# Global queries' scores in fp16 pairs: 32 columns of the array for each head

## The chip, the cores and the metric

The kernel runs on one core of a Trainium2 chip. The metric is device microseconds of one execution. The kernel before takes 972.75 us, the median of three runs (970.81 to 973.52).

## The reference

Attention with 8 batches, 8 heads, 512 local and 32 global positions of 64 elements, and behind it a feed-forward part with the function g = h * tanh(softplus(h)):

```python
k_all = np.concatenate([k_g, k_l], axis=2)
v_all = np.concatenate([v_g, v_l], axis=2)
s_g = scale * np.matmul(q_g, k_all.transpose(0, 1, 3, 2))   # 32 global queries against all 544 keys
out_g = np.matmul(sm(s_g), v_all)
s_ll = np.where(mask, scale * np.matmul(q_l, k_l.transpose(0, 1, 3, 2)), -1e9)   # |i - j| <= 32
s_lg = scale * np.matmul(q_l, k_g.transpose(0, 1, 3, 2))
out_l = np.matmul(sm(np.concatenate([s_lg, s_ll], axis=-1)), v_all)
x = np.concatenate([out_g, out_l], axis=2)      # as (8 * 544, 512)
h = x @ w_in                                    # 512 to 2048
out = (h * np.tanh(np.log1p(np.exp(h)))) @ w_out   # 2048 to 512
```

Here `sm` is the softmax. The change touches `s_g` alone: the scores of the 32 global queries of a head against its 32 global and 512 local keys.

## The kernel before

Heads go in pairs: 8 batches by 4 pairs are 32 head pairs `(b, hp)`. A pair's work is cut into four *units* of 128 local queries; in the third unit (`t == 2`) the global queries of the pair are worked as well. Beside the attention run the two products of the feed-forward part: `h` (line 869, 12 matmuls of 256 columns for half a step) and `o` (line 937, 6 of 512 columns). A block of 256 rows has eight such steps; 17 blocks make 136 steps.

fp32 operands are split into a high and a low fp16 part, so that a product of fp32 accuracy is a sum of fp16 matmuls. For the first eight head pairs (batches 0 and 1) the scores are taken straight from fp32 instead (`plain_s`). For the other 24 the keys are there as `ks` (high) and `kl` (low), and the queries hold the high part in one half of the partitions and the low part in the other, so that one matmul over 128 partitions gives two of the partial products.

The 24 sets of global scores are made by `g_scores` (from line 771), in two parts that go into two banks: part 0 has 32 columns of global keys and 256 of local ones, part 1 has 256 local ones. The stationary operand is a slice of `qgh`, whose 64 columns are 32 for either head; in the slice for head 0 the columns of head 1 are zeros, and the other way round. All four products (high and low keys, two heads) are added up in one region of 64 partitions: 0 to 31 for head 0, 32 to 63 for head 1. So a part has 4 matmuls for every range of columns, and a head pair 12: 8 of 256 columns and 4 of 32.

What follows a set: the row maximum (`g_max`, VectorE, line 791), Exp (`g_exp`, ScalarE, line 799), the normalized and split probabilities `gph` (VectorE, lines 807 to 811), a DMA transpose into `gpt` (line 482) and the product with the values `gu` (line 826).

No engine's order is written out by hand. Each piece of work is a task with the engine or engines that may do it, a duration in ns and what it reads and writes. `Plan.order` runs through the tasks with these durations, in priority order, and so fixes each engine's queue and, where two engines can do a task, which of them does it. A task of another table of functions (Exp or Mish) on ScalarE carries an `ACT_TABLE_LOAD`. The durations of `g_scores` are the second argument of its `pl.add(PE, ...)`, where `mm(n, cols)` stands for n matmuls of that many columns.

Of the kernel before, what the change touches and what calls it, by code (L numbers as in the profile page):

```python
# [48 lines left out]
PE, DVE, ACT, POOL, DMA = "PE", "DVE", "ACT", "POOL", "DMA"  # L49
# [174 lines left out]
def attn_mish_kernel(ctx: ExitStack, tc: tile.TileContext, qt, kt, qt0, kt0, mxs, vm, vg, qg, w1, w2, consts_in, out, w64):  # L224
    nc = tc.nc
    V, A, T, G = nc.vector, nc.scalar, nc.tensor, nc.gpsimd
# [17 lines left out]
    pl = Plan()  # L244
    X = pl.tile
# [44 lines left out]
    def mm(n, cols):  # L290
        return n * max(28, cols / 2.4)
# [175 lines left out]
    def plain_s(b, hp):  # L467
        return b * HP + hp < NPS

    def pair(b, hp, kind):  # L470

        return (kind, b, hp // 2), hp % 2
# [97 lines left out]
    def loc(k, j, n):  # L570

        a = k[:, 160 * j:160 * j + 64]
        return bass.AP(a.tensor, a.offset, [list(a.ap[0]), [160, n], [96, 2], list(a.ap[-1])])
# [54 lines left out]
    def bank(name):  # L628

        return [("h" if early else "sc", name)]  # L630
# [140 lines left out]
    def g_scores(b, hp, part):  # L771
        ks, kl, q, g = ("ks", b, hp), ("kl", b, hp), ("qgh", b), ("g", b, hp, part)

        def products(terms):
            a = 0 if part else 32
            for c0, n, rhs in ((a, 256, lambda k: loc(k, 2 * part, 2)), (0, 32, lambda k: k[:, GC:GC + 32]))[:2 - part]:
                for i, (a, k) in enumerate(terms):
                    T.matmul(X[g][:64, c0:c0 + n], a, rhs(k), start=(i == 0), stop=(i == len(terms) - 1))  # L778

        if plain_s(b, hp):  # L780
            kn, kp = pair(b, hp, "kn")
            pl.add(PE, mm(1, 1024) + 150 + (1 - part) * 90, lambda: products([(X["qgraw", b][:, 0, hp, :], X[kn][:, kp])]),
                   r=[[kn, kp], ("qgraw", b)], new=bank(g))
            return
        pl.add(PE, mm(4, 262) + 100 + (1 - part) * 110, lambda: products([(X[q][:, h, hp, :], X[k][:, h]) for k in (ks, kl) for h in range(2)]),
               r=[ks, kl, q], new=bank(g))

    def g_max(b, hp):
# [197 lines left out]
    def slot(u):  # L986
# [43 lines left out]
        if t == 2:  # L1030
            att(g_scores, b, hp, 0)
            att(g_scores, b, hp, 1)
            att(g_max, b, hp)
# [122 lines left out]
    for x in ORDER.split():  # L1156
        a, n = x[0], int(x[1:] or 0)
# [92 lines left out]
```

## Time and profile before

| | |
|---|---|
| median of three runs | 972.75 us |
| the profiled execution | 970.08 us, span 968.3 us |
| TensorE (PE) busy | 924.9 us, 96% |
| VectorE (DVE) busy | 677.3 us, 70% |
| ScalarE (ACT) busy | 660.2 us, 68% |
| mean granted TensorE clock | 0.979 |
| first and last start of a matmul of the 24 blocks | 213.5 and 812.3 us |

Line numbers are those of the listing above; PE is TensorE's matmuls, PEld its weight loads, which overlap them. A group's row gives the tiles and shapes, the count, the time in which any of them ran, the mean of one, and the idle time of the engine just before them. A shape such as `128*64 128x256` is a matmul over 128 partitions with 64 columns of weights that streams 256 columns.

### The profile page before, as it was taken

How to read it: one execution, taken by the hardware profiler on the slowest of the kernel's cores; microseconds unless marked ns; L12 is line 12 of the kernel's file. 1: busy time of each engine (PE TensorE's matmuls, PEld its weight loads, DVE VectorE, ACT ScalarE, POOL GpSimd, SP SyncE). 2: the span in 40 equal slices, each digit the busy share in tenths (PEclk: the TensorE clock that was granted, in tenths of full speed). 3: DMA queues.
4: the chain of work that ended last, by engine and by line, in shares of the span. 5: the costliest groups of instructions: out<-in, count | busy, mean ns of one | idle time of the engine just before them, and what ended most of it. 6: DMA issues, size and time to landing. Idle time of an engine off the chain costs nothing.

```text
span 968.3 us, 20617 instructions
## 1 busy us (share of the span) xinstructions
PE 924.9 (96%) x7988; PEld 644.6 (67%) x7988; DVE 677.3 (70%) x1782; ACT 660.2 (68%) x1301; POOL 15.8 (2%) x28
## 2 busy tenths in 40 slices
PE   6787999999999999999999999999999999999995
PEld 3554774667677677676777777777677777666663
DVE  6799989778899788766777778776777655322221
ACT  4657677687788788787878887878888887211110
POOL 2000000000000000000000000000000000000000
PEclk9977899999999999999999999999999999999998
DMA  8887549888999867756585676565767442100000
GB/s 271 245 299 220 151 118 211 192 184 227 236 220 250 168 137 189 162 139 130 135 171 132 145 163 146 131 138 123 187 119 155 75 101 52 34 1 23 1 22 22
DMA packets 214010, 141.00 MB, mean 146 GB/s; under 512 B 176664, under 2 KB 188184, under 8 KB 212888
## 3 DMA queue, kind: packets, MB, share of 16 engines
q1 hardware_dynamic: 213912, 139.69, 60.0%
q8 instruction: 62, 1.02, 0.5%
q14 instruction: 36, 0.29, 0.1%
HBM read 75.15 MB, written 8.91 MB: 87 GB/s over the span
## 4 chain that ended last, share of the span: by engine, by line
PE 70%; DVE 15%; DMA 8%; issue 2%; ACT 2%; SPq 1%; POOL 0%; DVEq 0%; ACTq 0%
PE h L869 28%; PE o L937 27%; DMA pt<-ph 3%; PE U L740 3%; PE g L778 3%; DMA gpt<-gph 3%; PE s L656 3%; PE s L649 2%; DVE P L662 2%; PE gu L826 1%; DMA vraw<-in_vm 1%; DVE G L925 1%; DVE W L407 1%; DVE W L459 1%; DVE vmx L497 1%
## 5 line engine op out<-in xcount | busy, mean ns | idle before, releaser
L937 PE MATMUL o<-W,G 128*128 128x512 f16 x1632 | 390.1, 380 | 0.0
L869 PE MATMUL h<-xh,W 128*128 128x256 f16 x2048 | 376.7, 273 | 2.2 <-ACT e L912 2.2
L869 PEld LDWEIGHTS <-W 128*128 128x128 f16 x3264 | 311.2, 98 | 66.5 <-issue 8.9
L869 PE MATMUL h<-xl,W 128*128 128x256 f16 x1024 | 279.6, 273 | 0.0
L937 PEld LDWEIGHTS <-G 128*128 128x128 f16 x1632 | 158.0, 98 | 148.2 <-issue 4.2
L912 ACT ACTIVATE e<-h,c 128x512 f32<-128x512 f32 (+1 forms) x137 | 92.6, 683 | 124.8 <-PE h L869 123.6
L671 ACT ACTIVATE P<-P,nm 128x192 f32<-128x192 f32 (+1 forms) x256 | 117.9, 461 | 42.6 <-DVE nm L662 39.6
L328 DVE TENSOR_SCALAR G<-e,c 128x512 f16<-128x512 f32 (+1 forms) x117 | 56.1, 481 | 118.2 <-ACT e L912 118.1
L662 DVE CUSTOM_DVE_ANT_0 P<-s,consts 128x192 f32<-128x192 f32 (+1 forms) x256 | 91.1, 367 | 57.1 <-PE s L656 50.6
L925 DVE SCALAR_TENSOR_TENSOR G<-e,c,G 128x512 f16<-128x512 f32 (+1 forms) x137 | 101.9, 744 | 2.6
L723 DVE SCALAR_TENSOR_TENSOR ph<-P,ph 128x384 f16<-128x384 f32 (+1 forms) x112 | 65.4, 585 | 49.1 <-ACT ph L326 48.6
L912 ACT ACT_TABLE_LOAD x74 | 94.9, 1283 | 1.3
L671 ACT ACT_TABLE_LOAD x66 | 84.7, 1283 | 1.2
L740 PEld LDWEIGHTS <-pt 96*128 96x128 f16 (+1 forms) x1536 | 62.4, 99 | 15.3 <-DMA pt<-ph 5.3
L326 ACT ACTIVATE ph<-P 128x384 f16<-128x384 f32 (+1 forms) x107 | 58.3, 546 | 8.6 <-DMA pt<-ph 5.8
L740 PE MATMUL U<-va,pt 128*128 128x64 f16 (+1 forms) x768 | 57.3, 195 | 4.1 <-DMA pt<-ph 3.2
L740 PE MATMUL U<-vc,pt 96*128 96x64 f16 x768 | 56.2, 194 | 0.0
L671 ACT ACTIVATION_READ_ACCUMULATOR P<-P,nm 128x1 f32 x256 | 47.9, 187 | 0.0
L799 ACT ACTIVATE gP<-g,gmx 64x288 f32<-64x288 f32 x64 | 30.3, 475 | 24.8 <-DVE gmx L794 24.6
L656 PEld LDWEIGHTS <-qs 128*128 128x128 f16 x384 | 34.9, 98 | 17.2 <-issue 0.9
L649 PE MATMUL s<-kn,qn 64*128 64x192 f32 (+1 forms) x128 | 37.2, 486 | 7.6 <-DMA qn<-in_qt 4.4
L656 PE MATMUL s<-ks,qs 128*128 128x192 f16 (+1 forms) x192 | 42.3, 254 | 0.2 <-ACT gP L799 0.2
(121 smaller groups left out, 961.4 us busy)
## 6 DMA issues: line engine op xcount, KB each, us to landing
kraw<-in_kt SPq DMA_DIRECT2D x24, 640.0 KB, 4.3
kn_m<-in_mxs SPq DMA_DIRECT2D x24, 544.0 KB, 4.8
qraw<-in_qt SPq DMA_DIRECT2D x24, 512.0 KB, 4.3
out<-ob SPq DMA_DIRECT2D x34, 256.0 KB, 2.4
vraw<-in_vm SPq DMA_DIRECT2D x8, 1024.0 KB, 6.0
wraw<-in_w SPq DMA_DIRECT2D x16, 512.0 KB, 5.0
W<-in_w SPq DMA_DIRECT2D x16, 512.0 KB, 6.7
vc<-vf SPq DMA_DIRECT2D x32, 128.0 KB, 2.4
```

What stands on the lines that cost most here:

```text
L326: A.activation(out=dst, in_=src, func=AF.Copy, scale=c)
L328: V.tensor_scalar(dst, src, c, None, ALU.mult)
L649: pl.add(PE, mm(1, 4 * w), lambda: T.matmul(X[s][:, :w], X[q][r, part, t * 128:(t + 1) * 128], X[k][r, part, c0:c0 + w], start=True, stop= ...
L656: T.matmul(X[s][:, :w], X[qs][:, h, t * 128:(t + 1) * 128], X[k][:, h, c0:c0 + w], start=(i == 0), stop=(i == 1))
L662: pl.add(DVE, 69 + 1.04 * w, lambda: V.tensor_tensor_reduce(out=X[P][:, h, :w], in0=X[s][:, :w], in1=mask[:, m0:m0 + w], scale=-SCALE, sca ...
L671: pl.add(ACT, 94 + 0.832 * w + 186, lambda: A.activation(out=X[P][:, h, :w], in_=X[P][:, h, :w], func=AF.Exp, bias=X[nm], scale=-1.0, accu ...
L723: pl.add(DVE, dve(n), lambda: V.scalar_tensor_tensor(p_part(X[ph], t, 1), p_src(X[P], t), PSC, p_part(X[ph], t, 0), ALU.mult, ALU.subtract ...
L740: T.matmul(X[u][:, t, h, :], X[pt][:k, p * 4 + h * 2 + c, :], X[vx][:k, t, vl, h * 64:(h + 1) * 64], start=(n == 0), stop=(n == 5))
L869: T.matmul(X[h][:, f * TB:(f + 1) * TB], wh(i, wl)[:, off:off + 128], X[x][:, d, o:o + TB], start=(n == 0), stop=(n == 11))
L912: chain(blk, i, ACT, 587, lambda a, z: A.activation(out=X[e][:, a:z], in_=hv(blk, i)[:, a:z], func=AF.Mish, bias=0.0, scale=X[c][:, 0:1]), ...
L925: chain(blk, i, DVE, 663, lambda a, z: V.scalar_tensor_tensor(gp(1, blk, i)[:, a:z], X[e][:, a:z], X["c", blk][:, 2:3], gp(0, blk, i)[:, a ...
L937: T.matmul(X[o], gp(g, blk, i)[:, f, t * 128:(t + 1) * 128], wh(8 + i, wl)[:, f * 512:(f + 1) * 512], start=(i == 0 and n == 0), stop=(i = ...
```

## The change

For the 24 fp16 head pairs, a head's products go to its own 32 columns of the array and its own 32 partitions of the bank, with only the 32 columns of `qgh` that hold that head's queries. They are issued in turns: high keys for head 0, high keys for head 1, low keys for head 0, low keys for head 1, for each range of columns. Each head's pair of products is a sum of its own with its own `start` and `stop`. The number of matmuls and weight loads stays the same, as does the tile `qgh`. The eight fp32 pairs issue what they issued before. The planner's durations for the two fp16 parts are changed with it.

```diff
-        def products(terms):
+        def products(*groups):
             a = 0 if part else 32
             for c0, n, rhs in ((a, 256, lambda k: loc(k, 2 * part, 2)), (0, 32, lambda k: k[:, GC:GC + 32]))[:2 - part]:
-                for i, (a, k) in enumerate(terms):
-                    T.matmul(X[g][:64, c0:c0 + n], a, rhs(k), start=(i == 0), stop=(i == len(terms) - 1))
+                for i in range(len(groups[0][2])):
+                    for p0, p1, terms in groups:
+                        a, k = terms[i]
+                        T.matmul(X[g][p0:p1, c0:c0 + n], a, rhs(k), start=(i == 0), stop=(i == len(terms) - 1))
...
-            pl.add(PE, mm(1, 1024) + 150 + (1 - part) * 90, lambda: products([(X["qgraw", b][:, 0, hp, :], X[kn][:, kp])]),
+            pl.add(PE, mm(1, 1024) + 150 + (1 - part) * 90, lambda: products((0, 64, [(X["qgraw", b][:, 0, hp, :], X[kn][:, kp])])),
                    r=[[kn, kp], ("qgraw", b)], new=bank(g))
             return
-        pl.add(PE, mm(4, 262) + 100 + (1 - part) * 110, lambda: products([(X[q][:, h, hp, :], X[k][:, h]) for k in (ks, kl) for h in range(2)]),
+        pl.add(PE, mm(2, 262) + 160 + (1 - part) * 80, lambda: products(*(
+            (h * 32, h * 32 + 32, [(X[q][:, h, hp, h * 32:h * 32 + 32], X[k][:, h]) for k in (ks, kl)]) for h in range(2))),
                r=[ks, kl, q], new=bank(g))
```

On TensorE, the first of the 24 blocks and what stands behind it. Before (`g_0_1` is part 1 of the head pair; rows in which both orders agree are left out):

```order
L778 LDWEIGHTS qgh_2695
L778 MATMUL g_0_1_2780<-kl_0_1909,qgh_2695 64x256
L937 LDWEIGHTS G_2605
L937 MATMUL o_0_2169<-W,G_2605 128x512
...
L869 LDWEIGHTS W
L869 MATMUL h_0_2804<-xh_1902,W 128x256
L869 LDWEIGHTS W
L869 MATMUL h_0_2804<-xl_1915,W 128x256
```

The same place with the change:

```order
L780 LDWEIGHTS qgh_2695
L780 MATMUL g_0_1_2780<-kl_0_1909,qgh_2695 32x256
L940 LDWEIGHTS G_2605
L940 MATMUL o_0_2169<-W,G_2605 128x512
...
L940 LDWEIGHTS G_2605
L940 MATMUL o_1_2231<-W,G_2605 128x512
L940 LDWEIGHTS G_2605
L940 MATMUL o_1_2231<-W,G_2605 128x512
...
L872 LDWEIGHTS W
L872 MATMUL h_0_2816<-xh_1902,W 128x256
```

The output of a matmul has 32 rows instead of 64. Behind the block both halves of an `o` step now come ahead of the next `h`, where before an `h` stood between them; this is the first row in which TensorE's queue differs, and from here on all queues are arranged anew.

On ScalarE, at the fourth head pair of batch 2 (`e` is Mish of `h`, `P` the Exp of local scores). Before:

```order
L912 ACTIVATE e_2_3768<-h_2_3693,c_2227 128x512
...
L671 ACT_TABLE_LOAD
L671 ACTIVATE P_74,sums_3_3710<-P_74,nm_3_1_0_3860 128x224
L671 ACTIVATE P_74,sums_3_3710<-P_74,nm_3_1_1_3877 128x224
L319 CAST xs_2_3895<-x_2_3881 128x512
L326 ACTIVATE ph_81<-P_74 128x2x224
L912 ACT_TABLE_LOAD
L912 ACTIVATE e_3_3934<-h_3_3789,c_2227 128x512
L671 ACT_TABLE_LOAD
L671 ACTIVATE P_75,sums_3_3710<-P_75,nm_3_2_0_3950 128x224
```

With the change:

```order
L915 ACTIVATE e_2_3782<-h_2_3710,c_2227 128x512
...
L915 ACTIVATE e_3_3855<-h_3_3784,c_2227 128x512
...
L671 ACT_TABLE_LOAD
L671 ACTIVATE P_74,sums_3_3726<-P_74,nm_3_1_0_3910 128x224
L671 ACTIVATE P_74,sums_3_3726<-P_74,nm_3_1_1_3918 128x224
L671 ACTIVATE P_75,sums_3_3726<-P_75,nm_3_2_0_3950 128x224
```

The Mish of step 3 has moved ahead of the Exp of unit 1, so that two table loads fall away here. Over the whole program there are 116 loads for `e` and `P`, where there were 140, and 11 instead of 20 casts to `G` on ScalarE (VectorE has the nine others).

## The prediction

> **What bounds the kernel now.** I read the page's engine totals first, then the busy time by stage, then what TensorE waits for, then the matmuls around one of the changed blocks in order of time.
>
> ```profile
> span 968.3 us, 20617 instructions
> PE 924.9 (96%) x7988; PEld 644.6 (67%) x7988; DVE 677.3 (70%) x1782; ACT 660.2 (68%) x1301; POOL 15.8 (2%) x28
> ...
> core 0: us, PE busy (x) PEld busy (x) DVE busy (x) ACT busy (x) POOL busy (x), PEclk, DMA share, GB/s
> 100.00:213.00 113.00, 109.96 (x950) 73.76 (x949) 98.45 (x255) 79.17 (x166) 1.67 (x4) 0.99 0.71 171
> ...
> 213.00:812.00 599.00, 592.68 (x5474) 424.75 (x5470) 454.66 (x1218) 492.25 (x936) 7.06 (x10) 1.00 0.69 155
> 812.00:968.30 156.30, 146.38 (x1032) 97.67 (x1028) 41.03 (x76) 28.79 (x47) 0.00 (x0) 0.98 0.07 19
> ```
>
> TensorE is the bound. A busy PE need not be at its peak, but from 213 to 812 us, the stage in which all the changed blocks lie, it leaves only 599 - 592.68 = 6.3 us empty, at a granted clock of 1.00; VectorE is busy for 76% of that stage and ScalarE for 82%. After 812 us there are only the two products of the feed-forward part, back to back until the output goes out. So the end moves by whatever TensorE's queue gains or loses in the middle stage, provided that the other engines still feed it. What it waits for there is short:
>
> ```profile
> engine line waited for: us in total, times, longest us
> PE gu L826 <- DMA gpt<-gph: 3.5, 5, 1.2
> PE U L740 <- DMA pt<-ph: 2.4, 2, 2.0
> PE s L656 <- ACT gP L799: 0.2, 1, 0.2
> ```
>
> These are transposed probabilities that come late by DMA; none of the waits is for the global scores themselves. The changed work is in these groups:
>
> ```profile
> L778 PEld LDWEIGHTS <-qgh 128*64 128x64 f16 x288 | 22.2, 111 | 4.3 <-issue 3.8 <-ACT P L671 0.2
> ...
> L778 PE MATMUL g<-ks,qgh 128*64 128x256 f16 x96 | 19.0, 280 | 0.0
> L778 PE MATMUL g<-kl,qgh 128*64 128x256 f16 x96 | 18.3, 273 | 0.0
> ```
>
> The mean of 273 to 280 ns is a latency: matmuls are pipelined, so their price is the distance between starts. One block, in order of time:
>
> ```profile
> start us, us, engine line op out<-in xcount [idle before <-releaser]
> 426.85 0.27 PE L869 MATMUL h<-xl,W 128*128 128x256 f16 x1
> 426.96 0.27 PE L869 MATMUL h<-xh,W 128*128 128x256 f16 x1
> 427.16 0.41 PE L778 MATMUL g<-ks,qgh 128*64 128x256 f16 x2
> 427.41 0.38 PE L778 MATMUL g<-kl,qgh 128*64 128x256 f16 x2
> 427.62 0.21 PE L778 MATMUL g<-ks,qgh 128*64 128x32 f16 x2
> 427.68 0.21 PE L778 MATMUL g<-kl,qgh 128*64 128x32 f16 x2
> 427.75 0.39 PE L778 MATMUL g<-ks,qgh 128*64 128x256 f16 x2
> 427.97 0.38 PE L778 MATMUL g<-kl,qgh 128*64 128x256 f16 x2
> 428.28 0.28 PE L869 MATMUL h<-xh,W 128*128 128x256 f16 x1
> ```
>
> From the last h matmul ahead of the block (426.96) to the first behind it (428.28) are 1.32 us; two h matmuls in sequence stand 0.11 apart (426.85 to 426.96). So the block costs TensorE **1.21 us**. Its 8 wide matmuls step by 0.107 (427.41 to 427.62 for two): 0.86. Its 4 narrow ones step by 0.032 (427.62 to 427.75 for four): 0.13. The remaining 0.22 is spent on going in and out: 426.96 to 427.16 is 0.20 instead of 0.11, the last two take 0.31 instead of 0.21, and the first step inside is 0.03 too long. The 96 wide `ks` records are four to each of **24 blocks** (six batches of four head pairs; the first eight pairs take the fp32 path): 24 x 1.21 = 29.0 us, 3% of the span.
>
> **The change part by part.** Nothing is added to or taken from the instruction count: 12 weight loads and 12 matmuls per block, as before. Each load and output now has 32 columns, not 64, and two neighbours in the queue belong to two heads, in columns 0 to 31 and 32 to 63. If the array runs both at once, a pair of wide matmuls costs one step. The arithmetic is the same but for products with zeros.
>
> *Overlap.* No two column groups work side by side in the trace of before. The nearest row is of the fp32 scores, where the two heads of a pair use the two row halves of the array:
>
> ```profile
> 103.44 0.27 PE L869 MATMUL h<-xh,W 128*128 128x256 f16 x1
> 103.65 0.59 PE L649 MATMUL s<-kn,qn 64*128 64x192 f32 x2
> 104.17 0.28 PE L869 MATMUL h<-xh,W 128*128 128x256 f16 x1
> ...
> 144.14 0.65 PE L649 MATMUL s<-kn,qn 64*128 64x224 f32 x4
> 144.72 1.04 PE L937 MATMUL o<-W,G 128*128 128x512 f16 x4
> ```
>
> One head (two records, 192 columns) holds the array from 103.65 to 104.17, 0.52 us; both heads (four records, 224 columns) hold it from 144.14 to 144.72, 0.58 us. In sequence the two would need some 2 x 0.52 x 224/192 = 1.21. So on this chip neighbours in the queue on different halves run together, and I take the same for column groups. The Trainium skill, "TensorE: Matmul & The Clock Gate", Part 3 (Measured speedup vs the span model), gives 2.38 times for three column tiles of 32 and 512 columns each, and some 4 ns for every further tile; by it, as an estimate, a pair of wide ones would cost a step and 4 ns.
>
> Wide ones: 8 x 0.107 becomes 4 x 0.107 = 0.43. Bounds: 0.86 with no overlap, 0.43 with all of it.
>
> *Narrow ones.* At the pace of the wide ones, 32 columns would take 0.107 x 32/256 = 0.013; they take 0.032. So something other than the streaming sets that step, and pairing need not shorten it. I keep 4 x 0.032 = 0.13; the other bound is half, 0.065.
>
> *Second of a pair.* It may start one such smallest step, 0.032, after the first. Between pairs this is hidden, since the next matmul of the first head can already run; it shows where a row of wide ones ends, twice a block: 0.06. Bounds: 0, and all four wide pairs, 0.13.
>
> *In and out.* 0.22, as before: the array still goes from full width to a narrow tile and back once a block, and weight loads keep their number.
>
> Sum of a block: 0.43 + 0.13 + 0.06 + 0.22 = 0.84, so **0.37 us less**, x 24 = **8.9 us**. Best bound: 0.43 + 0.065 + 0.22 = 0.715, 0.495 less, 11.9 us. Lower bound with overlap: 0.43 + 0.13 + 0.13 + 0.22 = 0.91, 0.30 less, 7.2 us.
>
> *The order.* The planner now counts a block as shorter, so all that follows 213 us on TensorE, VectorE, ScalarE and the DMA queue is rearranged; before the first such block nothing moves. ScalarE has 116 table loads ahead of Exp and Mish, not 140, and nine fewer G casts, which VectorE takes.
>
> ```profile
> L912 ACT ACT_TABLE_LOAD x68 | 87.2, 1283 | 1.2
> L671 ACT ACT_TABLE_LOAD x63 | 80.8, 1283 | 1.1
> ...
> L328 DVE TENSOR_SCALAR G<-e,c 128x512 f16<-128x512 f32 x115 | 55.4, 483 | 115.4 <-ACT e L912 115.3
> ```
>
> That is 24 x 1.283 = 30.8 us off ScalarE's 492 in the stage (the counts of these rows are of the stage alone). TensorE waits for ScalarE for 0.2 us there, so I count it at nothing by itself; it is room for the shorter stage, in which ScalarE has to do the rest in some 590 us. VectorE gets nine casts of 0.48 us, 4.3, and has 144 us free in the stage. The DMA transposes are as many as before, but must be ready 8.9 us sooner at the end of the stage; they are what would be late next. Waits of TensorE: between 0 and, if they double, 12.6 us, against 6.3 now; I keep 6.3, since the two reasons that I see, a lighter ScalarE and a faster TensorE, pull apart. The blocks with the array switched twice, split by a piece of other work, fall from two to one; at 0.2 us I leave this out.
>
> The profiled execution took 970.08 us with a span of 968.3; 8.9 less is 961.2. The median of the runs, 972.75, lies 2.7 above the profiled execution, and the forecast is made against the median: 972.75 - 8.9 = **963.9 us**.
>
> **The rivals.**
>
> *The array empties at every change of column group (slower).* Going from h to g costs 0.20 - 0.11 = 0.09 extra. Were that due at each of the 11 changes inside a block, nothing would overlap and 24 x 11 x 0.09 = 23.8 us would be added: 996.5. It decides from 0.011 us a change (24 x 11 x 0.011 = 2.9 us). For it: entry and exit do cost this much whenever the tile's width changes. Against: the row halves change at each record of the fp32 scores, and the two heads of 144.14 lose nothing by it. 0.07.
>
> *No overlap (the change doesn't do what it says).* Weights of both heads lie on all 128 rows. If the second head's load waits for the first head's matmul, the pair is serial and the block stays at 1.21: 972.75. Against: in the block above the loads do go on beside matmuls that use the same rows, for 12 loads of 0.111 us, 1.33 in sequence, fit in a block of 1.21. The Trainium skill, "TensorE: Matmul & The Clock Gate", Part 3 (The mechanism), says that a weight load overlaps running matmuls only where the row group differs, which speaks for this rival; the rows above already contradict it for loads to one column group. 0.07.
>
> *The new order gives it back.* The stage 100 to 213 us has 113 - 109.96 = 3.04 us without TensorE, 2.7%. At that rate the middle stage would have 16.1, 9.8 more than now: 972.75 - 8.9 + 9.8 = 973.7. For it: every dependent piece after 213 us is placed anew, and the transposes are already late at seven places. Against: feed-forward work is queued throughout and fills most holes, and ScalarE is lighter. 0.08.
>
> *More than forecast.* Best bound of the block and half of the 6.3 us of waits gone with the table loads: 972.75 - 11.9 - 3.1 = 957.8. 0.05.
>
> **How the numbers follow.** My forecast has the rest, 0.73. About 0.3%, 2.9 us, can be told from no change here, so faster means below 969.8. Faster: 0.73 + 0.05 = 0.78. Same: no overlap 0.07 and 0.07 of the order's 0.08, 0.14. Slower: 0.07 + 0.01 = 0.08. Low end: the best bound, 960.9, less the 1.9 by which the lowest run lies under the median, 959.0. High end: 7.2 us gained and waits doubled, 972.75 - 7.2 + 6.3 = 971.9; with no overlap just outside.
>
> **What would show it.** In a block's order of time the wide matmuls of two heads should start nearly together, with 0.1 us to the next pair, and from the last matmul ahead to the first behind should be 0.95, not 1.32. The last block should end some 9 us before 812. The narrow ones tell whether their step halves. Starts 0.2 us apart inside a block would be the emptied array; an unchanged 1.32 no overlap; a short block with an unmoved end the order, and then TensorE's waits in the middle stage must have grown past 12 us and name what is late.

## The result, and the profile after

The changed kernel takes 966.28 us (median of six runs, 965.14 to 967.7) where the kernel before takes 972.23 (six runs, 970.81 to 973.52): a ratio of **0.994, interval 0.9926 to 0.9953**, 6.0 us. 963.9 had been forecast. The profiled execution took 966.51 us, its span is 964.7; that is 3.6 less than the span of before, whose profiled execution lay under all of its timed runs. Experiments are therefore judged by medians and ratios, profiles by their stages.

The page's totals, and then the stage from 213 to 812 us as it was cut for the kernel before (columns as there: length, busy time of PE, PEld, DVE, ACT and POOL, granted clock, DMA):

```profile
span 964.7 us, 20600 instructions
PE 914.6 (95%) x7988; PEld 630.5 (65%) x7988; DVE 680.7 (71%) x1789; ACT 623.4 (65%) x1270; POOL 15.8 (2%) x28
```

```profile
213.00:812.00 599.00, 585.58 (x5506) 412.22 (x5504) 461.39 (x1236) 459.31 (x915) 7.17 (x10) 1.00 0.69 156
```

TensorE stands still for 599 - 585.58 = 13.4 us of it, where it was 6.3. ScalarE's busy time fell from 492 to 459 us, as the table loads had said. The block that was shown of before, here at another head pair, in order of time:

```profile
422.59 0.27 PE L872 MATMUL h<-xl,W 128*128 128x256 f16 x1
422.70 0.27 PE L872 MATMUL h<-xh,W 128*128 128x256 f16 x1
422.90 0.29 PE L780 MATMUL g<-ks,qgh 128*32 128x256 f16 x2
423.02 0.28 PE L780 MATMUL g<-kl,qgh 128*32 128x256 f16 x2
423.13 0.18 PE L780 MATMUL g<-ks,qgh 128*32 128x32 f16 x2
423.16 0.18 PE L780 MATMUL g<-kl,qgh 128*32 128x32 f16 x2
423.19 0.27 PE L780 MATMUL g<-ks,qgh 128*32 128x256 f16 x2
423.30 0.27 PE L780 MATMUL g<-kl,qgh 128*32 128x256 f16 x2
423.50 0.28 PE L872 MATMUL h<-xh,W 128*128 128x256 f16 x1
```

Each row now is a pair, one matmul of either head. Two wide ones together last 0.29 or less, where one alone lasts 0.27: in the trace they start 3 ns apart. The next pair follows after 0.11 to 0.12, where a single one took 0.11 before. From the last h ahead (422.70) to the first behind (423.50) are **0.80 us instead of 1.32**; the blocks of the other head pairs that stand whole between two `h` matmuls have the same two values at the median. 24 x 0.52 = 12.5 us are gained, more than the 11.9 of the forecast's best bound. What TensorE waits for in the stage tells where half of it went:

```profile
PE gu L829 <- DMA gpt<-gph: 8.6, 9, 1.6
PE U L740 <- DMA pt<-ph: 3.3, 5, 1.4
PE g L780 <- DVE nm L662: 0.6, 1, 0.6
PE o L940 <- ACT ob L326: 0.2, 1, 0.2
```

The waits of `gu`, the product with the values that closes the chain of the same global queries, rose from 3.5 to 8.6 us, and all the standing still from 6.3 to 13.4. 12.5 less 7.1 is 5.4. In the two profiled executions the time from the first start of a matmul of the 24 blocks to the last fell from 598.8 us (213.5 to 812.3) to 594.0 (214.3 to 808.3), by 4.8, and the medians differ by 6.0.

### The profile page after: what moved, and what is told of

Its sections match the earlier page's. It is cut to its first block, busy times and chain, and to the rows that moved or that the text cites. A ratio compares the mean times of both kernels' runs of the same rounds, so it can differ in the third digit from the quotient of the medians.

```text
span 964.7 us, 20600 instructions
## 1 busy us (share of the span) xinstructions
PE 914.6 (95%) x7988; PEld 630.5 (65%) x7988; DVE 680.7 (71%) x1789; ACT 623.4 (65%) x1270; POOL 15.8 (2%) x28
## 4 chain that ended last, share of the span: by engine, by line
PE 52%; DVE 23%; DMA 13%; ACT 4%; issue 4%; SPq 1%; DVEq 0%; ACTq 0%
PE o L940 23%; PE h L872 19%; DMA gpt<-gph 5%; DMA pt<-ph 3%; DMA vraw<-in_vm 3%; PE U L740 3%; DVE P L662 2%; PE s L656 2%; DMA kn_m<-in_mxs 2%; DVE kl L594 2%; PE s L649 2%; DVE G L928 2%; PE gu L829 2%; DVE gmx L794 1%; DVE W L407 1%
## 5 line engine op out<-in xcount | busy, mean ns | idle before, releaser
L328 DVE TENSOR_SCALAR G<-e,c 128x512 f16<-128x512 f32 (+1 forms) x126 | 60.4, 480 | 128.7 <-ACT e L915 128.6
L656 PE MATMUL s<-kl,qs 128*128 128x192 f16 (+1 forms) x192 | 42.2, 252 | 0.0
```

What stands on the lines that cost most here:

```text
L328: V.tensor_scalar(dst, src, c, None, ALU.mult)
L656: T.matmul(X[s][:, :w], X[qs][:, h, t * 128:(t + 1) * 128], X[k][:, h, c0:c0 + w], start=(i == 0), stop=(i == 1))
```

## The experiments

Two theories were set against each other. **A**: the shorter block by itself makes the waits. TensorE's queue from the start of the scores to `gu` has a fixed content; it got shorter by the 0.52 us that the block lost, while the chain beside it (row maximum, Exp, split, transpose) did not, so `gu` is reached before its transpose has landed. **B**: the new order, which the planner made for shorter durations, is worse by itself and gives back what the block gains.

**The changed products in the order of before.** The planner's durations are put back; every queue then stands as before.

```diff
-        pl.add(PE, mm(2, 262) + 160 + (1 - part) * 80, lambda: products(*(
+        pl.add(PE, mm(4, 262) + 100 + (1 - part) * 110, lambda: products(*(
```

> The changed products with the planner's durations of before, so that every queue stands as before. Theory A (the shorter block brings 24 x 0.52 = 12.5 us, and TensorE gives about half of it back at gu, because its own work between the scores and gu shrank while the chain scores, maximum, Exp, transpose did not): the block falls to 0.80 us between its neighbours as in the changed kernel, the waits of gu for gpt grow from 3.5 to about 8 us here too, and the time is 5 to 8 us under before (ratio 0.992 to 0.995). Theory B (the new order gives it back, by itself): waits stay near 3.5 us and the time is 11 to 13 us under before (ratio 0.987 to 0.989).

Measured 968.47 us beside 971.4 of before: 0.9967 (0.9949 to 0.9985), 2.9 us. The stage and TensorE's waits in it:

```profile
213.00:812.00 599.00, 586.16 (x5510) 413.43 (x5509) 457.84 (x1230) 495.33 (x946) 6.81 (x10) 1.00 0.71 156
```

```profile
PE gu L829 <- DMA gpt<-gph: 8.1, 12, 1.4
PE U L740 <- DMA pt<-ph: 1.9, 3, 1.0
PE s L656 <- ACT gP L802: 1.9, 3, 0.8
```

12.8 us of standing still, 8.1 of them before `gu`, without any new order. B's range is excluded. The gain is smaller than A gave it, and TensorE now also waits for the Exp of global scores (`s` behind `gP`, 1.9 instead of 0.2); local and global scores share a ring of three banks.

Why the chain did not move up with the shorter block can be read from the order of time on VectorE. At one head pair, before (its block starts at 427.16) and in this run (at 425.24):

```profile
428.10 0.56 DVE L723 SCALAR_TENSOR_TENSOR ph<-P,ph 128x384 f16<-128x384 f32 x1
428.58 0.44 DVE L791 TENSOR_REDUCE gmx<-g 64x1 f32<-64x288 f32 x1
```

```profile
426.18 0.56 DVE L723 SCALAR_TENSOR_TENSOR ph<-P,ph 128x384 f16<-128x384 f32 x1
426.66 0.44 DVE L794 TENSOR_REDUCE gmx<-g 64x1 f32<-64x288 f32 x1
```

The first row maximum starts 1.42 us after the block's start in both: it waits for its turn on VectorE, not for the scores. At the median of the 24 blocks it starts 1.33 us after the block's start and the transpose is issued after 8.67 us, in both runs. From issue to landing the transposes take 3.7 us at the median before and 3.8 here, so they are hardly slower themselves. The block's 0.52 us is missing on TensorE's side alone.

**The products of before in the new order.** The converse: 64 columns with zeros, the durations of the change.

```diff
-        pl.add(PE, mm(4, 262) + 100 + (1 - part) * 110, lambda: products([(X[q][:, h, hp, :], X[k][:, h]) for k in (ks, kl) for h in range(2)]),
+        pl.add(PE, mm(2, 262) + 160 + (1 - part) * 80, lambda: products([(X[q][:, h, hp, :], X[k][:, h]) for k in (ks, kl) for h in range(2)]),
```

> The products of before (64 columns with zeros) with the planner's new durations, so that every queue stands as in the changed kernel. Theory A: the block costs 1.21 us, TensorE's work between scores and gu is as long as before and the waits of gu stay at 3 to 5 us; time within 2 us of before (ratio 0.998 to 1.002). Theory B: the waits of the new order, 8.6 us at gu, are there in full beside the old block, so 5 to 6 us over before (ratio 1.005 to 1.006).

Measured 969.72 us, ratio 0.998 (0.9962 to 0.9999).

```profile
213.00:812.00 599.00, 593.12 (x5482) 424.63 (x5480) 460.10 (x1230) 457.49 (x908) 7.18 (x10) 1.00 0.69 155
```

```profile
PE gu L826 <- DMA gpt<-gph: 3.7, 6, 1.0
```

5.9 us of standing still, as before. The new order costs nothing by itself; if anything it brings 1 or 2 us. B, which had 1.005 to 1.006, is out: the waits belong to the short block.

**The change once more**, beside these on the same chip.

> The changed kernel once more, on the chip of the other three, so that they can be set against it: ratio 0.993 to 0.995, block 0.80 us between neighbours, gu waits near 8.6 us.

Measured 967.13 us, 0.9958 (0.9941 to 0.9976), a little outside what was expected; the waits of `gu` were 11.8 us in this execution, and the stage's row shows 16.0 us of standing still:

```profile
213.00:812.00 599.00, 583.03 (x5481) 410.64 (x5479) 459.10 (x1230) 456.60 (x907) 7.17 (x10) 1.00 0.70 155
```

The gain in this comparison is 4.3 us where the first showed 6.0; the two intervals overlap. One kernel stood still for 13.4 us in one execution and 16.0 in another, so a sum made from single profiles is good to some 3 us. The medians of this chip separate the two parts of the change: the short block brings 2.9 us in the old order (971.4 to 968.47) and 2.6 in the new one (969.72 to 967.13), the order 1.7 and 1.3, each uncertain by some 2 us. So here only about a quarter of the block's 12.5 us reaches the end, and the order adds some of the gain. For the last step the profiles agree: 12.5 less the waits that grew from 5.9 to 16.0 leaves 2.4. For the first they don't: 12.5 less the growth from 6.3 to 12.8 would leave 6.0, where the medians show 2.9; the profiled execution of that run took 965.63 us, 2.8 less than its median.

**Head by head.** The products of the change, but not in turns.

```diff
-                for i in range(len(groups[0][2])):
-                    for p0, p1, terms in groups:
-                        a, k = terms[i]
+                for p0, p1, terms in groups:
+                    for i, (a, k) in enumerate(terms):
```

> As the changed kernel, but the products are issued head by head (high keys and low keys for head 0, then both for head 1) and not in turns. If two neighbours overlap only where they lie in different column groups, the two of one head step by 0.109 us, the first of the next head starts some 3 ns after the last of the one before, and the last of each run stands alone: the block costs about 0.92 us, not 0.69 or 1.21, and the time is 3 to 5 us under before (ratio 0.995 to 0.997). If a matmul of 32 columns were cheaper by itself, the block would stay at 0.69 and the time at that of the changed kernel (ratio 0.994).

Both expectations were wrong in their reasons. The time is 968.32 us, 0.9963 (0.9944 to 0.9983), inside the first one's range and, within the noise, that of the change; the block is as long as the second one had it. The queue holds, for a range of columns, `ks` and `kl` of head 0 and then `ks` and `kl` of head 1. In order of time:

```profile
374.28 0.27 PE L871 MATMUL h<-xh,W 128*128 128x256 f16 x1
374.48 0.29 PE L779 MATMUL g<-ks,qgh 128*32 128x256 f16 x2
374.60 0.28 PE L779 MATMUL g<-kl,qgh 128*32 128x256 f16 x2
374.71 0.19 PE L779 MATMUL g<-ks,qgh 128*32 128x32 f16 x2
374.74 0.18 PE L779 MATMUL g<-kl,qgh 128*32 128x32 f16 x2
374.76 0.28 PE L779 MATMUL g<-ks,qgh 128*32 128x256 f16 x2
374.87 0.28 PE L779 MATMUL g<-kl,qgh 128*32 128x256 f16 x2
375.08 0.28 PE L871 MATMUL h<-xh,W 128*128 128x256 f16 x1
```

Two `ks` start together, 7 ns apart in the trace, then two `kl`: the `ks` of head 1 has passed the `kl` of head 0, which stands ahead of it in the queue and waits for its own columns. The block takes 0.80 us between its neighbours (0.69 beyond a step), as with the products in turns. So it isn't the neighbour in the queue that has to lie in the other columns.

**All of a part for one head, then for the other.** How far ahead does a matmul pass?

```diff
-            for c0, n, rhs in (...)[:2 - part]:
-                for i in range(len(groups[0][2])):
-                    for p0, p1, terms in groups:
...
+            for p0, p1, terms in groups:
+                for c0, n, rhs in (...)[:2 - part]:
+                    for i, (st, k) in enumerate(terms):
...
```

> The changed kernel with all four products of head 0 in a part (high and low keys for the local columns, then for the global ones) ahead of all four of head 1. The run head by head showed matmuls of the two heads starting in pairs though two of one head stood next to each other in the queue. If TensorE starts a matmul of a free column group ahead of one that waits for its own, four in sequence don't matter either, and the block stays at 0.80 us between its neighbours with starts in pairs. If only the next one or two can pass, part 0 becomes longer by about one wide step or more and the block takes 0.9 to 1.05 us.

One execution, 966.61 us; its time decides nothing, its trace does. Part 0 now has four matmuls of head 0 ahead of the first of head 1.

```profile
395.77 0.27 PE L871 MATMUL h<-xh,W 128*128 128x256 f16 x1
395.98 0.30 PE L779 MATMUL g<-ks,qgh 128*32 128x256 f16 x2
396.10 0.29 PE L779 MATMUL g<-kl,qgh 128*32 128x256 f16 x2
396.20 0.19 PE L779 MATMUL g<-ks,qgh 128*32 128x32 f16 x2
...
396.58 0.28 PE L871 MATMUL h<-xh,W 128*128 128x256 f16 x1
```

0.81 us, and the two wide `ks` start 13 ns apart: at least three matmuls that wait are passed.

**A later gu.** If A holds, the gain comes back when the planner puts more feed-forward work between the scores and `gu`. It does so if it thinks that the transpose takes longer; the transpose itself stays the same.

```diff
-        turn(160, lambda: X[pt], lambda: X[ph].rearrange("p a k -> p (a k)"), r=[ph], new=[("gpt", pt)])
+        pl.add(DMA, (1250, 3002), lambda: nc.sync.dma_start_transpose(X[pt], X[ph].rearrange("p a k -> p (a k)")), r=[ph], new=[("gpt", pt)])
```

`turn` gives 250 + 160 x 4.7 = 1002 ns; 3002 is 2000 more.

> The changed kernel with 2 us more in the planner's duration for the DMA transpose of gpt, so that the planner puts gu behind more feed-forward work (the transpose itself is the same). Theory A (what is given back is TensorE standing before gu, because its own work between scores and gu is too short for the chain): waits of gu for gpt fall from 8.6 to 11.8 us to under 4, those at other places stay, time 4 to 7 us under the changed kernel (ratio to before 0.988 to 0.991). Rival C (the waits only move, since the transposes are late at the DMA queue as such): all waits of TensorE in the middle stage stay near 12 us and the time at that of the changed kernel (ratio 0.994 to 0.996).

With 4002, 3000 more in place of 2000:

> The same with 3 us more. Theory A: waits of gu near 0 to 1 us, time as with 2 us more or 1 to 2 us under it. Rival C: as the changed kernel, 0.994 to 0.996.

And 3002 with the products of before:

> The products of before (64 columns with zeros) in the order of the run with 2 us more, as a control: the distance between scores and gu was nearly enough for the long block, so a later gu has little to bring. Theory A: waits of gu from 3.7 to under 1 us and 1 to 3 us under the run with old products in the new order (ratio to before 0.995 to 0.998), and some 10 to 12 us over the changed products in the same order. If the later gu brought as much here (5 us or more), the gain would be one of the order alone.

Measured 969.01 us (0.9984, interval 0.9972 to 0.9996), 974.99 us (1.0037, 1.0023 to 1.0051) and 976.54 us (1.0058, 1.0041 to 1.0076), in this order, beside 970.57 of before. Every expectation of A for the time failed, although the waits of `gu` did go:

```profile
PE U L740 <- DMA pt<-ph: 3.2, 6, 1.0
PE h L872 <- ACT e L915: 1.4, 2, 0.8
...
PE gu L829 <- DMA gpt<-gph: 0.3, 1, 0.3
```

That is the run with 2 us more. The reason is ahead of the stage: two rows of this run, its whole first stage and the middle one, and then the same two of the changed kernel:

```profile
0.00:225.50 225.50, 191.46 (x1500) 125.22 (x1501) 182.48 (x493) 138.63 (x315) 9.24 (x18) 0.86 0.72 198
225.50:812.00 586.50, 579.54 (x5463) 411.66 (x5464) 459.69 (x1233) 434.34 (x888) 8.33 (x10) 0.99 0.71 159
```

```profile
0.00:214.20 214.20, 187.79 (x1500) 123.75 (x1500) 182.32 (x490) 139.59 (x322) 8.60 (x18) 0.91 0.76 210
214.20:812.00 597.80, 584.42 (x5489) 411.58 (x5488) 460.19 (x1235) 458.14 (x911) 7.17 (x10) 1.00 0.69 156
```

The longer duration held for the fp32 pairs too and rearranged the first stage: the first fp16 block starts at 225.6 us, not 214.3, with 34 us without TensorE, not 26, and the mean granted clock is 0.86, not 0.91. The middle stage has 7.0 us of standing still instead of 13.4. What was won behind the first block was lost ahead of it. In the other two runs the first block starts late as well, at 229.1 and 225.4 us. With the same order the two products are 976.54 - 969.01 = 7.5 us apart, not 10 to 12.

**A later gu for the fp16 pairs alone.** The duration is now `250 + 160 * 4.7 + (0 if plain_s(b, hp) else 2000)`; TensorE's queue is that of the change until behind the first fp16 block, where the first `gu` of the fp16 pairs comes later.

> As the run with 2 us more in the planner's duration for the transpose of gpt, but for the 24 fp16 head pairs alone: that run also rearranged the first stage, where the first block came 12 us later, and lost there what it won behind it. Now all queues stand as in the changed kernel until behind the first block. Theory A: first block near 213 us, waits of gu under 2 us, all waits of TensorE in the middle stage 4 to 8 us instead of 13 to 16, time 4 to 8 us under the changed kernel (ratio to before 0.986 to 0.991). Rival C (something else holds the middle stage): no better than the changed kernel, 0.994 to 0.996.

With 1000 in place of 2000:

> The same with 1 us more instead of 2. Theory A: waits of gu 2 to 5 us, time between the changed kernel and the run with 2 us (0.988 to 0.993). Rival C: 0.994 to 0.996.

With 2000 and the products of before:

> The products of before (64 columns with zeros) in the order of the run with 2 us more for the fp16 pairs. Theory A: this order leaves no wait at gu for either block, so the two differ by the whole price of the block, 24 x 0.52 = 12.5 us: 10 to 13 us over the run with the changed products in this order, near the time of before (ratio 0.997 to 1.002). If the difference of the two is again only 4 to 6 us, the block's price reaches the end only in part for a reason that gu is not.

Measured beside 971.98 of before: **961.45 us, 0.9898 (0.9879 to 0.9918)** with 2 us; 962.89 us, 0.9915 (0.9892 to 0.9938) with 1 us, where `gu` waits for 1.3 us; 968.69 us, 0.9958 (0.9941 to 0.9975) with 2 us and the old products. The stage and the waits with 2 us and the changed products:

```profile
213.00:812.00 599.00, 589.90 (x5559) 418.38 (x5557) 464.88 (x1245) 443.85 (x905) 7.69 (x10) 1.00 0.70 157
```

```profile
PE U L740 <- DMA pt<-ph: 2.6, 6, 0.6
PE h L872 <- ACT e L915: 2.6, 1, 2.6
PE s L656 <- DVE nm L662: 2.2, 2, 1.9
PE o L940 <- ACT ob L326: 1.1, 2, 0.9
PE gu L829 <- DMA gpt<-gph: 0.4, 1, 0.4
```

The same order with the products of before:

```profile
213.00:812.00 599.00, 594.14 (x5502) 427.02 (x5501) 463.24 (x1239) 442.23 (x899) 7.70 (x10) 1.00 0.69 156
```

```profile
PE h L869 <- ACT e L912: 2.7, 1, 2.7
PE s L656 <- DVE nm L662: 1.4, 1, 1.4
PE U L740 <- DMA pt<-ph: 0.6, 3, 0.2
```

A stands: with `gu` behind enough work its waits are gone, 0.4 instead of 8.6 us, and the kernel is 10.5 us faster than before, a ratio of 0.9898 where the changed kernel had 0.994 and 0.9958. That is the best version here. Part of it is the order alone: with the old products it brings 3.3 us (971.98 to 968.69). All waits of the stage came to 9.1 us, more than the 4 to 8 expected. And the control did not come out as A had it. In an order that leaves no wait at `gu` with either product, the block's 12.5 us show at the end as 968.69 - 961.45 = 7.2, not as 10 to 13. The stage's rows account for it: 9.1 us of standing still with the short block, 4.9 with the long one, 4.2 more, in small pieces before `U`, `s` and `o`. 12.5 - 4.2 = 8.3, against the 7.2 measured. The waits of `U` are for transposes, as those of `gu` are; that these are chains of the same kind, which the long block had covered, is a reading that no run tests by itself. So `gu` was the largest of the places that give the gain back, not the only one.

## Why the prediction was right, and where it was off

**Direction, range and place** held: faster, inside 959.0 to 971.9, by a shorter block in a stage that TensorE bounds. The gain was 6.0 us where 8.9 had been forecast, and this is the balance of two terms that were each mis-sized, in opposite directions, and each beyond its stated bounds: 0.52 us a block where the best bound was 0.495, and 13.4 us of waits where the upper bound was 12.6. That the sum came near is luck.

**The block was priced too dear.** 0.37 us less had been taken, and 0.52 were measured. *Overlap* was right: a wide pair takes one step. *Narrow ones* was the wrong bound: their step of 0.032 had been read as a floor for each matmul, but two of different column groups share it (423.13, 423.16 and 423.19 for two pairs), 0.06 us and not 0.13. *Second of a pair* was wrong as well: it starts 3 ns after the first, not 32, and costs next to nothing. *In and out* was 0.22 and came to some 0.19 (422.70 to 422.90, and 423.30 to 423.50, each 0.20 where a step is 0.11, and one step of 0.12).

**The waits were held at 6.3 us and came to 13.4.** This is the step that failed: "the two reasons that I see, a lighter ScalarE and a faster TensorE, pull apart". ScalarE did become lighter by 33 us in the stage, and that took next to nothing off TensorE's waits: with the long block in the new order, ScalarE just as light, they were 5.9 us, and the time 1.7 us under before. The prediction had itself counted the lighter ScalarE at nothing elsewhere. The waits that came are those of the faster TensorE. What the prediction had named as "what would be late next", the transposes, is what became late; their price was set to nothing. Of the rivals, "the new order gives it back" had the size nearly right, 9.8 us of more waits against 7.1 measured, and the reason wrong: the two crossed runs show the waits with the old order and the short block (12.8 us), and not with the new order and the long block (5.9 us). The prediction's sign for that rival, waits past 12 us, therefore came true without it: the sign could not tell a worse order from a shorter block. One row was misread without effect: the `G` casts counted 115 are those of the whole program, and only their mean of 0.48 us entered the sum.

**The other rivals** fell as argued. No step inside a block is longer than before, so the array doesn't empty between column groups. Overlap is there. The line for which the prediction cites the Trainium skill, "TensorE: Matmul & The Clock Gate", Part 3 (The mechanism), that a weight load overlaps running matmuls only where the row group differs, does not hold in these traces; the same section lets a load also go ahead when it is for the background weight buffer, and which buffer a load takes no run here shows. The loads of the changed blocks:

```profile
L780 PEld LDWEIGHTS <-qgh 128*32 128x32 f16 x288 | 9.0, 95 | 5.8 <-issue 5.2
```

Twelve of 0.095 us are 1.14 in sequence, all on the same 128 rows as the matmuls beside them, and the block takes 0.80 with its matmuls. In the block of before, where nothing is paired, a load of 0.110 starts 1 to 2 ns after a wide matmul does and lasts until the next one starts, 0.109 later.

## What to carry to other kernels

When a piece of work on the bounding engine is made cheaper, look for a later instruction on the same engine that needs its result by way of other engines: the cheaper piece shortens the distance in the queue but not the chain, whose first step may wait for its turn on another engine and not for the cheaper piece, and the rest of the gain has to be fetched by putting other work between the two. The profile of before says how near that is: `gu` already waited at five places for 3.5 us, and with the block shortened in the same order it was twelve places and 8.1 us. A planner's duration is changed only for the tasks in question: a longer one for all pairs spoiled a stage that was not.

## What the runs showed of the hardware

TensorE does not start matmuls strictly in the order of its queue. With the products head by head, and with four of head 0 ahead of four of head 1, the two heads' matmuls still started in pairs, 7 and 13 ns apart, and the block took 0.80 and 0.81 us against 0.80 in turns. The Trainium skill, "TensorE: Matmul & The Clock Gate", Part 3 (The mechanism), calls matmuls "strict FIFO, no reordering"; for matmuls in different column groups these two runs show otherwise.

Going from an array of full width to a tile of 32 columns and back costs about 0.09 us each way (0.20 between starts where 0.11 is the step), the same as with 64 columns (426.96 to 427.16 in the block of before). With a block of 0.80 us that is nearly a quarter of it, and what is left to win there lies in doing two head pairs at one go, which was not tried.
